# Output projection of blocks 1 to 8 by one level of Strassen's product, with the sums of h on VectorE

## Chip, cores, metric

The kernel runs on one core of one Trainium2 chip. The metric is device time in microseconds (us); quoted times are medians of several executions. The span in a profile is some 1.8 us shorter than the time of the same execution. Faster or slower is given at 2%.

## The reference

Linear attention over 8 batches of 8 heads, 576 rows of 64, then a GEGLU block on the 4608 x 512 result:

```python
q_s = softmax(q, axis=-1); k_s = softmax(k, axis=2)           # per head
x   = (q_s @ (k_s^T @ v)) laid out as 4608 x 512
g, val = x @ w_gate, x @ w_val                                # 512 -> 1536
out = (gelu(g) * val) @ w_out                                 # 1536 -> 512
```

## The kernel before

Rows are handled in blocks of 512: blocks 0 to 7 are one batch each (512 of its 576 rows), block 8 gathers the remaining 64 rows of all; the order is 0 to 6, 8, 7. A block runs 12 steps `fi` (128 of the 1536 hidden features each: four matmuls for the gate, four for the value, a gelu on ScalarE, a product on VectorE that writes the f16 slice `ht`) and then the output projection. The attention of later batches rides between these steps, by a plan `at(block, FI or NS, index, work)`; instructions of an engine run in program order. In the plan's names, exp and norm are the exponentials and the normalisation of a softmax, kv is the product of k and v, x that of q with kv, and FI or NS says whether the work rides behind a step `fi` or in the output projection.

```python
ps_big = tile_pool("ps_big", bufs=6, PSUM); ps_att = tile_pool("ps_att", bufs=2, PSUM)   # 8 banks
...
def gate(psg, psv):
    gl = ffn.tile([P, 512], f32, tag="gl")
    nc.scalar.activation(out=gl, in_=psg, func=ACTF.Gelu)
    ht = htp.tile([P, 512], f16, tag="ht")
    nc.vector.scalar_tensor_tensor(out=ht, in0=psv, scalar=_H_SCALE, in1=gl, op0=mult, op1=mult)
    return ht
...
def mm_out(psy, hts, ns, fis):
    for fi in fis:
        nc.tensor.matmul(psy, hts[fi][:, ns*P:(ns+1)*P], wo_sb[:, fi, :],
                         start=(fi == 0), stop=(fi == NFI - 1))
...
# plan, block 1 and later
at(1, FI, 3, L(exp, "q", 2), L(norm, 2, 0, "pool"))          # norm = reduce + reciprocal on VectorE,
...                                                          # multiply on GpSimd ("pool")
at(1, FI, 7, L(exp, "k", 2, 0, 4), L(cast_v, 2, 0, H))       # cast_v: f32 -> f16 on GpSimd
at(1, FI, 11, L(load_batch, 3), L(exp, "k", 2, 4, 8), L(exp, "q", 3), L(exp, "k", 3), ...)
at(1, NS, 0, L(unit_kv4, 2)); at(1, NS, 1, L(unit_x4, 2, ("dve", "dve"), 1))   # block 2's x
at(2, FI, 7, L(norm_rem0))
for b in range(2, B):
    at(b, FI, 0, L(load_batch, b + 2))
    at(b, FI, 11, L(exp, "q", b + 2), L(exp, "k", b + 2), L(cast_v, b + 2, 0, H))
    ...
# per block, b > 0
for ns in range(4):
    psy = ps_big.tile([P, C], f32, tag="mm")
    mm_out(psy, hts, ns, range(6));  ride(b, NS, 10 + ns)
    mm_out(psy, hts, ns, range(6, 12)); evac(b, ns, psy); ride(b, NS, ns)
```

The softmax here doesn't subtract the row's maximum and nothing guards it: scores larger than these inputs give would overflow.

## Time and profile before

| | before |
|---|---|
| time | 313.39 us (313.31 to 313.39, 3 runs) |
| TensorE / VectorE / ScalarE / GpSimd busy | 97 / 54 / 45 / 17% of the span of 311.7 us |
| output projection of one block | 48 matmuls of 512 columns, 10.4 us |

A group's row is: line, engine, operation, output <- inputs, shapes, count | busy us, mean ns of one | idle us just before, and what ended it. A timeline row is: start us, duration us, engine, line, operation, count, and in brackets the idle time before it with its releaser. A record of a matmul lasts longer than its share of a stream (379 ns for 216), because neighbours overlap. The lines themselves stand in the prediction.

### The profile page before, as it was taken

What the parts mean: (1) busy time and instruction counts of PE and PEld (TensorE: products, weight loads), DVE (VectorE), ACT (ScalarE), POOL (GpSimd) and SP (SyncE); (2) the same over time, 40 slices, a digit from 0 to 9 for tenths busy, and PEclk for the clock granted to TensorE, in tenths of its full rate; (3) what the DMA queues carried; (4) which work ended last, traced back from release to release, by engine and by line L of the source; (5) the groups of instructions that cost most, each with busy time, mean ns of one, the idle gap of its engine ahead of it and who ended that gap; (6) DMA issues with size and microseconds to landing.
All of it is one profiled execution on the core that took longest, in us unless ns stands there. A gap on an engine that the chain in (4) does not pass through costs nothing.

```text
span 311.7 us, 4689 instructions
## 1 busy us (share of the span) xinstructions
PE 302.9 (97%) x1813; PEld 140.6 (45%) x1813; DVE 168.8 (54%) x293; ACT 139.6 (45%) x181; POOL 54.0 (17%) x67
## 2 busy tenths in 40 slices
PE   3999999999999999999999999999999999999995
PEld 1544455444444444444444444444444444444444
DVE  2944386483686478437853686358643443324331
ACT  4763475994843743366335633474330333013300
POOL 2667451071083100110003000300000000000000
PEclk9999999999999999999999999999999999999999
DMA  7999999609999018901693149512210200140002
GB/s 227 372 383 393 401 386 388 182 2 262 375 337 241 0 69 269 334 14 67 191 349 69 67 127 386 97 43 93 54 33 34 103 0 0 36 101 0 0 36 101
DMA packets 55189, 51.61 MB, mean 166 GB/s; under 512 B 18560, under 2 KB 50688, under 8 KB 55168
## 3 DMA queue, kind: packets, MB, share of 16 engines
q1 hardware_dynamic: 53440, 49.68, 49.6%
q10 hardware_dynamic: 1728, 1.64, 1.7%
q8 instruction: 14, 0.23, 0.3%
q14 instruction: 7, 0.06, 0.1%
HBM read 37.75 MB, written 9.44 MB: 151 GB/s over the span
## 4 chain that ended last, share of the span: by engine, by line
PE 95%; DMA 2%; DVE 2%; ACT 0%; issue 0%; ACTq 0%
PE psg L406 30%; PE psv L406 30%; PE psy L481 29%; DMA qt<-in_q_dram 2%; PE pskv L281 1%; PE psl L502 1%; PE psx L369 1%; DVE rq L186 1%; PE psx L348 1%; DVE eq L195 0%; PE pskv L222 0%; PE pst L306 0%; PE psxr L369 0%; ACT eq L158 0%; PE pskv L258 0%; DVE eqt L138 0%
## 5 line engine op out<-in xcount | busy, mean ns | idle before, releaser
L411 ACT ACTIVATE gl<-psg 128x512 f32<-128x512 f32 x108 | 63.6, 598 | 122.9 <-PE psg L406 122.5
L413 DVE SCALAR_TENSOR_TENSOR ht<-psv,gl 128x512 f16<-128x512 f32 x108 | 74.0, 689 | 81.5 <-PE psv L406 77.4
L406 PE MATMUL psg<-xt,wg_sb 128*128 128x512 f16 x384 | 100.5, 379 | 0.0
L406 PE MATMUL psv<-xt,wv_sb 128*128 128x512 f16 x384 | 100.5, 379 | 0.0
L481 PE MATMUL psy<-wo_sb,ht 128*128 128x512 f16 x420 | 93.9, 379 | 0.0
L406 PEld LDWEIGHTS <-wv_sb 128*128 128x128 f16 x432 | 42.1, 98 | 50.8 <-issue 0.2
L406 PEld LDWEIGHTS <-wg_sb 128*128 128x128 f16 x432 | 42.1, 98 | 50.3
L481 PEld LDWEIGHTS <-ht 128*128 128x128 f16 x420 | 40.5, 98 | 48.4 <-issue 0.8
L530 DVE TENSOR_SCALAR yo<-psy 128x512 f32<-128x512 f32 x30 | 20.6, 688 | 32.4 <-PE psy L481 32.4
L134 POOL CAST v<-vt 128x640 f16<-128x640 f32 x26 | 18.2, 740 | 108.9 <-DMA vt<-in_v_dram 108.9
L176 DVE TENSOR_REDUCE rq<-eq 128x10 f32<-128x640 f16 x28 | 22.7, 811 | 5.4 <-ACT eq L158 4.9
L158 ACT ACTIVATE eq<-qt 128x2560 f16<-128x2560 f32 (+2 forms) x10 | 18.5, 1864 | 6.8 <-DMA qt<-in_q_dram 6.8
L158 ACT ACTIVATE ek<-kt 128x1280 f16<-128x1280 f32 (+1 forms) x11 | 19.1, 1747 | 3.9 <-DMA kt<-in_k_dram 3.8
L195 POOL TENSOR_TENSOR eq<-eq,rrq 128x640 f16<-128x640 f16 (+1 forms) x11 | 14.3, 1300 | 25.4 <-DVE rrq L178 17.1
L195 DVE TENSOR_TENSOR eq<-eq,rrq 128x640 f16<-128x640 f16 (+1 forms) x21 | 17.3, 822 | 0.2
L406 PE MATMUL psg<-xtr,wg_sb 128*128 128x512 f16 x48 | 12.3, 379 | 0.0
L406 PE MATMUL psv<-xtr,wv_sb 128*128 128x512 f16 x48 | 12.3, 379 | 0.0
L138 DVE CAST xt<-psx 128x512 f16<-128x512 f32 (+1 forms) x17 | 10.7, 668 | 2.0 <-PE psx L348 1.8
L398 PE MATMUL pswarm<-warm,ident 128*128 128x512 f16 x20 | 6.9, 501 | 4.9 <-ACT warm L553 4.9
L158 ACT ACT_TABLE_LOAD x8 | 10.3, 1283 | 0.8 <-DMA qt<-in_q_dram 0.7
L136 ACT CAST xt<-psx 128x512 f16<-128x512 f32 (+1 forms) x16 | 8.6, 574 | 2.4 <-PE psx L348 2.2
L136 ACT CAST xtr<-psxr 128x128 f16<-128x128 f32 (+1 forms) x6 | 1.6, 283 | 17.8 <-PE psxr L369 15.3
(67 smaller groups left out, 111.0 us busy)
## 6 DMA issues: line engine op xcount, KB each, us to landing
out_dram<-yo SPq DMA_DIRECT2D x12, 512.0 KB, 3.6
kt<-in_k_dram SPq DMA_DIRECT2D x7, 640.0 KB, 7.1
vt<-in_v_dram SPq DMA_DIRECT2D x7, 640.0 KB, 8.7
qt<-in_q_dram SPq DMA_DIRECT2D x7, 640.0 KB, 5.6
qt<-in_q_dram SPq DMA_DIRECT2D x8, 512.0 KB, 6.2
wost<-in_moe_w_out_dram SPq DMA_DIRECT2D x6, 512.0 KB, 7.9
kt<-in_k_dram SPq DMA_DIRECT2D x6, 512.0 KB, 7.8
vt<-in_v_dram SPq DMA_DIRECT2D x6, 512.0 KB, 9.4
```

Of the source, the lines that this page charges most:

```text
L134: nc.gpsimd.tensor_copy(out=dst, in_=src)
L136: nc.scalar.copy(out=dst, in_=src)
L138: nc.vector.tensor_copy(out=dst, in_=src)
L158: nc.scalar.activation(out=dst[:, n0:NC, h0 * D:h1 * D].rearrange(o, d=D, **({"t": 2} if b >= QUAD else {})), in_=heads(tiles[(nm, b)], b, ...
L176: nc.vector.reduce_sum(rq, e, axis=mybir.AxisListType.X)
L195: (nc.gpsimd if eng == "pool" else nc.vector).tensor_tensor(out=e, in0=e, in1=rrq.unsqueeze(-1).to_broadcast((P, n, 2, D)), op=ALU.mult)
L398: nc.tensor.matmul(ps, ident, warm, start=True, stop=True)
L406: nc.tensor.matmul(ps, w[:, ci, fi * P:(fi + 1) * P], xt[:, ci, :], start=(ci == 0), stop=(ci == HP - 1))
L411: nc.scalar.activation(out=gl, in_=psg, func=ACTF.Gelu)
L413: nc.vector.scalar_tensor_tensor(out=ht, in0=psv, scalar=_H_SCALE, in1=gl, op0=ALU.mult, op1=ALU.mult)
L481: nc.tensor.matmul(psy, hts[fi][:, ns * P:(ns + 1) * P], wo_sb[:, fi, :], start=(fi == 0), stop=(fi == NFI - 1))
L530: nc.vector.tensor_scalar(out=yo, in0=psy, scalar1=1.0 / _H_SCALE, scalar2=None, op0=ALU.mult)
```

## The change

Split h and w_out into halves along both axes. One level of Strassen's product (in Winograd's form, with shared sums) replaces 8 half-size products by 7, at the price of sums of h halves (four per pair of slices, on VectorE in each of blocks 1 to 8), sums of w_out halves (four, once, in block 1) and more traffic at the eviction. With h's halves a11 (features 0 to 5, rows 0 to 255), a12 (features 6 to 11), a21, a22 (the same for rows 256 to 511):

```diff
+    ring = [f"mm{i}" for i in range(6)]          # banks handed out in fixed turn; some held across products
+    ht = const.tile([P, NFI, 512], f16)          # one tile for all of h
+    def sum_w(i):                                # tw1 = b12-b11, tw2 = b22-tw1, tw3 = b22-b12, tw4 = b21-tw2
+        nc.vector.tensor_tensor(out=t, in0=a, in1=b, op=ALU.subtract)          # 128 x 1536 f16
+    def sum_h(j0, j1, which):                    # s1 = a21+a22, s2 = s1-a11, a21 <- a11-a21, s4 = a12-s2
+        for i in which: nc.vector.tensor_tensor(out=o, in0=a, in1=b, op=op)    # (j1-j0) x 256 f16
+    SUMS = {7: (0, 2), 9: (2, 4), 10: (4, 5)}    # after these fi; slice 5 after the last gate
+    def out_strassen(b, last):                   # a, c, b: PSUM banks; snap: scaled copy to SBUF
+        product(1, ps["a"], True);  s1 = snap("a"); sum_h(5, 6, (3, 4))
+        product(5, ps["c"], True);  s5 = snap("c")
+        product(6, ps["a"], False); s2 = snap("a"); ride(b, NS, 2)
+        product(3, ps["c"], False); add("c", s2, 0, 1)
+        product(7, ps["a"], False); add("a", s5, 1, 1); ride(b, NS, 4)
+        product(2, ps["b"], True);  add("b", s1, 0, 0); store_rows(b, 0, yo[0])
+        product(4, ps["a"], False)               # evicted by ScalarE
...
+    for i in range(4): at(1, FI, 3 + i, L(sum_w, i + 1))
-    at(1, NS, 0, L(unit_kv4, 2))
-    at(1, NS, 1, L(unit_x4, 2, ("dve", "dve"), 1))
+    at(1, NS, 2, L(unit_kv4, 2))
+    at(1, NS, 4, L(unit_x4, 2, ("act", "dve"), 1))
...
-                at(*((b, FI, hp) if n == 3 else (b - 1, NS, hp)), L(norm_sum, n, hp))
-                at(b, FI, hp, L(norm_mul, n, hp, "pool" if n == 3 else "dve"))
+                at(b, FI, hp, L(norm_sum, n, hp), L(norm_mul, n, hp, "pool"))
...
+            if b > 0 and fi in SUMS: sum_h(*SUMS[fi], (1, 2, 3, 4))
```

A product is 6 x 2 matmuls of 256 columns, so a block has 84 of them. Below, the seam of a block is the stretch from its last gates into its first products, where the last sums of h and the snaps are due.

More of the change, by code (lines that the diff above doesn't have):

```diff
@@ L56, with big, let_go, bank @@
     yop = ctx.enter_context(tc.tile_pool(name="yop", bufs=2))
-    htp = ctx.enter_context(tc.tile_pool(name="htp", bufs=13))
-    ps_big = ctx.enter_context(tc.tile_pool(name="ps_big", bufs=6, space=bass.MemoryType.PSUM))
+    ps_big = ctx.enter_context(tc.tile_pool(name="ps_big", bufs=1, space=bass.MemoryType.PSUM))
     ps_att = ctx.enter_context(tc.tile_pool(name="ps_att", bufs=2, space=bass.MemoryType.PSUM))
     ctx.enter_context(tc.manual_schedule())
+    ring = [f"mm{i}" for i in range(6)]
+    held = {}
+    def big(shape, dt, name, hold=False):
+        tag = ring.pop(0)
+        t = ps_big.tile(shape, dt, name=name, tag=tag)
+        if hold:
+            held[id(t)] = (t, tag)
+        else:
+            ring.append(tag)
+        return t
+    def let_go(t):
+        ring.append(held.pop(id(t))[1])
+    def bank(shape, name, spare):
+        return big(shape, f32, name) if spare else ps_att.tile(shape, f32, name=name, tag="att")
     warm = const.tile([P, 512], f16)
@@ L74 @@
     xtr = const.tile([P, HP, B * REM], f16)
+    ht = const.tile([P, NFI, 512], f16)
+    s4 = const.tile([P, NO, 256], f16)
     q0r = const.tile([64, H, D], f32)
@@ L240, in ksum_mm @@
     def ksum_mm(g):
-        st[("pks", g)] = ps_big.tile([P, 2], f32, name="pks", tag="mm")
+        st[("pks", g)] = big([P, 2], f32, "pks")
         for j in range(2):
@@ L252, in kv0_mm @@
     def kv0_mm(hp):
-        ps = ps_big.tile([P, D], f32, name="pskv0", tag="mm")
+        ps = big([P, D], f32, "pskv0")
         st[("pskv0", hp)] = ps
@@ L271, in unit_kv, with unit_kv4 @@
         kv_norm(b, g)
-    def unit_kv4(b, big=False):
-        ps = (ps_big if big else ps_att).tile([P, HP, VW], f32, name="pskv",
-                                              tag="mm" if big else "att")
+    def unit_kv4(b, spare=False):
+        ps = bank([P, HP, VW], "pskv", spare)
         for hp in range(HP):
@@ L342, in get_xt, with unit_x @@
         return st[(b, "xt")]
-    def unit_x(b, hp, eng="act", big=False):
+    def unit_x(b, hp, eng="act", spare=False):
         xt = get_xt(b)
-        psx = (ps_big if big else ps_att).tile([P, MAIN], f32, name="psx",
-                                               tag="mm" if big else "att")
+        psx = bank([P, MAIN], "psx", spare)
         nc.tensor.matmul(psx, st[(b, "kv", hp)].rearrange("p h e -> p (h e)"),
@@ L355, in unit_x_halves @@
             c = slice(i * MAIN // 2, (i + 1) * MAIN // 2)
-            psx = ps_big.tile([P, MAIN // 2], f32, name="psx", tag="mm")
+            psx = big([P, MAIN // 2], f32, "psx")
             nc.tensor.matmul(psx, st[(b, "kv", hp)].rearrange("p h e -> p (h e)"),
@@ L386, in unit_x4 @@
         for i in range(2):
-            ps = [ps_big.tile([P, MAIN], f32, name="psx", tag="mm") for _ in range(2)]
+            ps = [big([P, MAIN], f32, "psx") for _ in range(2)]
             for hp in (2 * i, 2 * i + 1):
@@ L391, in unit_x4 @@
                 copy_on(eng, xt[:, i + 2 * s, :], ps[s])
-    pswarm = ps_big.tile([P, 512], f32, name="pswarm", tag="mm")
+    pswarm = big([P, 512], f32, "pswarm")
     def warm_pe(n):
@@ L407, in mm_gv, with gate @@
                              start=(ci == 0), stop=(ci == HP - 1))
-    def gate(psg, psv):
+    def gate(psg, psv, fi):
         gl = ffn.tile([P, 512], f32, name="gl", tag="gl")
         nc.scalar.activation(out=gl, in_=psg, func=ACTF.Gelu)
-        ht = htp.tile([P, 512], f16, name="ht", tag="ht")
         nc.vector.scalar_tensor_tensor(
-            out=ht, in0=psv, scalar=_H_SCALE, in1=gl, op0=ALU.mult, op1=ALU.mult)
-        return ht
+            out=ht[:, fi, :], in0=psv, scalar=_H_SCALE, in1=gl, op0=ALU.mult, op1=ALU.mult)
     def ffn_fi(xt, fi, spare=False):
-        pool, tag = (ps_att, "att") if spare else (ps_big, "mm")
-        psg = pool.tile([P, 512], f32, name="psg", tag=tag)
+        psg = bank([P, 512], "psg", not spare)
         mm_gv(psg, wg_sb, xt, fi, range(HP))
-        psv = pool.tile([P, 512], f32, name="psv", tag=tag)
+        psv = bank([P, 512], "psv", not spare)
         mm_gv(psv, wv_sb, xt, fi, range(HP))
-        return gate(psg, psv)
+        gate(psg, psv, fi)
     def ffn_first(xt, after):
@@ L428, in ffn_first @@
         for fi in range(len(after)):
-            psg = ps_big.tile([P, 512], f32, name="psg", tag="mm")
-            psv = ps_big.tile([P, 512], f32, name="psv", tag="mm")
+            psg = big([P, 512], f32, "psg")
+            psv = big([P, 512], f32, "psv")
             if fi == 0:
@@ L443, in ffn_first @@
             mm_gv(psv, wv_sb, xt, fi, [2])
-        hts = []
         for fi, (psg, psv) in enumerate(ps):
@@ L447, in ffn_first @@
             mm_gv(psv, wv_sb, xt, fi, [3])
-            hts.append(gate(psg, psv))
-        return hts
+            gate(psg, psv, fi)
     def ffn_first0(xt, xs):
@@ L455, in ffn_first0 @@
             for nm in ("g", "v"):
-                ps[(nm, fi)] = ps_big.tile([P, 512], f32, name="ps" + nm, tag="mm")
+                ps[(nm, fi)] = big([P, 512], f32, "ps" + nm)
         def go(fi, cis):
@@ L469, in ffn_first0, with mm_out @@
         go(1, (2,))
-        hts = []
         for fi in range(2):
             go(fi, (3,))
-            hts.append(gate(ps[("g", fi)], ps[("v", fi)]))
-        return hts
+            gate(ps[("g", fi)], ps[("v", fi)], fi)
     yo_t = {}
     order = list(range(B - 1)) + [B, B - 1]
-    def mm_out(psy, hts, ns, fis):
+    def mm_out(psy, ns, fis):
         for fi in fis:
-            nc.tensor.matmul(psy, hts[fi][:, ns * P:(ns + 1) * P], wo_sb[:, fi, :],
+            nc.tensor.matmul(psy, ht[:, fi, ns * P:(ns + 1) * P], wo_sb[:, fi, :],
                              start=(fi == 0), stop=(fi == NFI - 1))
@@ L492, in store @@
                                   ap=[[pm, nm], [NM * pn, 2]] + last), in_=src)
-    def last_rows(b, hts, ns):
-        cuts = ((0, 256), (256, 384), (384, 512))
-        ps = [ps_big.tile([P, c1 - c0], f32, name="psl", tag="mm") for c0, c1 in cuts]
-        for part in ((0,), (1, 2)):
-            for fi in range(NFI):
-                for i in part:
-                    c0, c1 = cuts[i]
-                    nc.tensor.matmul(ps[i], hts[fi][:, ns * P:(ns + 1) * P], wo_sb[:, fi, c0:c1],
-                                     start=(fi == 0), stop=(fi == NFI - 1))
-            for i in part:
-                c0, c1 = cuts[i]
-                yl = yop.tile([P, c1 - c0], f32, name=f"yl{i}", tag=f"yl{i}", bufs=1)
-                if i < 2:
-                    nc.vector.tensor_scalar(out=yl, in0=ps[i], scalar1=1.0 / _H_SCALE,
-                                            scalar2=None, op0=ALU.mult)
-                else:
-                    nc.scalar.activation(out=yl, in_=ps[i], func=ACTF.Copy, scale=1.0 / _H_SCALE)
-                store(nc.scalar if i == 2 else nc.sync, yl, b, ns, ns + 1, c0, c1)
+    tw = {}
@@ new lines, in sum_w, with make_s @@
+    def sum_w(i):
+        t = wstp.tile([P, NO, 256], f16, name=f"tw{i}", tag="wst")
+        b11, b12 = wo_sb[:, 0:NO, 0:256], wo_sb[:, 0:NO, 256:512]
+        b21, b22 = wo_sb[:, NO:NFI, 0:256], wo_sb[:, NO:NFI, 256:512]
+        a, b = {1: (b12, b11), 2: (b22, tw.get(1)), 3: (b22, b12), 4: (b21, tw.get(2))}[i]
+        nc.vector.tensor_tensor(out=t, in0=a, in1=b, op=ALU.subtract)
+        tw[i] = t
+    sh = {}
+    def make_s():
+        for i in (1, 2):
+            sh[i] = wstp.tile([P, NO, 256], f16, name=f"sh{i}", tag="wst")
@@ new lines, in sum_h @@
+    def sum_h(j0, j1, which):
+        a11, a21 = ht[:, j0:j1, 0:256], ht[:, j0:j1, 256:512]
+        a12, a22 = ht[:, NO + j0:NO + j1, 0:256], ht[:, NO + j0:NO + j1, 256:512]
+        s1, s2 = sh[1][:, j0:j1], sh[2][:, j0:j1]
+        for i in which:
+            o, a, b, op = {1: (s1, a21, a22, ALU.add), 2: (s2, s1, a11, ALU.subtract),
+                           3: (a21, a11, a21, ALU.subtract),
+                           4: (s4[:, j0:j1], a12, s2, ALU.subtract)}[i]
+            nc.vector.tensor_tensor(out=o, in0=a, in1=b, op=op)
@@ new lines, with product @@
+    SUMS = {7: (0, 2), 9: (2, 4), 10: (4, 5)}
+    def product(i, ps, first, ts=(0, 1)):
+        for j in range(NO):
+            for t in ts:
+                c0, c1 = slice(t * P, (t + 1) * P), slice(256 + t * P, 256 + (t + 1) * P)
+                a = {1: ht[:, j, c0], 2: ht[:, NO + j, c0], 3: s4[:, j, c0], 4: ht[:, NO + j, c1],
+                     5: sh[1][:, j, c0], 6: sh[2][:, j, c0], 7: ht[:, j, c1]}[i]
+                w = {1: wo_sb[:, j, 0:256], 2: wo_sb[:, NO + j, 0:256],
+                     3: wo_sb[:, NO + j, 256:512]}.get(i)
+                if w is None:
+                    w = tw[{4: 4, 5: 1, 6: 2, 7: 3}[i]][:, j]
+                nc.tensor.matmul(ps[t], a, w, start=(first and j == 0 and (
+                    t == ts[0] or ps[t].tensor is not ps[ts[0]].tensor)),
+                                 stop=(j == NO - 1), skip_group_check=True)
@@ new lines, in out_strassen, with get, parts, snap @@
+    def out_strassen(b, last):
+        yo = [yop.tile([P, 2, C], f32, name="yo", tag="yo") for _ in range(2)]
+        c = (slice(0, 256), slice(256, 512))
+        ps, tiles_ = {}, {}
+        def get(nm):
+            if last:
+                tiles_[nm] = [big([P, 256], f32, "ps" + nm, True) for _ in range(2)]
+                ps[nm] = [x for x in tiles_[nm]]
+            else:
+                tiles_[nm] = [big([P, 2, 256], f32, "ps" + nm, True)]
+                ps[nm] = [tiles_[nm][0][:, t] for t in range(2)]
+        def parts(nm):
+            return [(0, ps[nm][0]), (1, ps[nm][1])] if last else [(slice(0, 2), tiles_[nm][0])]
+        def snap(nm):
+            sn = ffn.tile([P, 2, 256], f32, name="sn", tag="gl")
+            for n, (t, src) in enumerate(parts(nm)):
+                if n:
+                    nc.scalar.activation(out=sn[:, t], in_=src, func=ACTF.Copy, scale=1.0 / _H_SCALE)
+                else:
+                    nc.vector.tensor_scalar(out=sn[:, t], in0=src, scalar1=1.0 / _H_SCALE,
+                                            scalar2=None, op0=ALU.mult)
+            return sn
+        def add(nm, sn, half, col):
+            for t, src in parts(nm):
+                nc.vector.scalar_tensor_tensor(
+                    out=yo[half][:, t, c[col]], in0=src, scalar=1.0 / _H_SCALE,
+                    in1=sn[:, t], op0=ALU.mult, op1=ALU.add)
+        get("a")
+        product(1, ps["a"], True)
+        s1 = snap("a")
+        sum_h(NO - 1, NO, (3, 4))
+        get("c")
+        product(5, ps["c"], True)
+        s5 = snap("c")
+        product(6, ps["a"], False)
+        s2 = snap("a")
+        ride(b, NS, 2)
+        product(3, ps["c"], False)
+        add("c", s2, 0, 1)
+        for x in tiles_["c"]:
+            let_go(x)
+        product(7, ps["a"], False)
+        add("a", s5, 1, 1)
+        ride(b, NS, 4)
+        if last:
+            for t in range(2):
+                store(nc.sync, yo[1][:, t, c[1]], b, 2 + t, 3 + t, 256, 512)
+        get("b")
+        product(2, ps["b"], True)
+        add("b", s1, 0, 0)
+        store_rows(b, 0, yo[0])
+        for x in tiles_["b"]:
+            let_go(x)
+        for ts in ((0,), (1,)) if last else ((0, 1),):
+            product(4, ps["a"], False, ts)
+            if ts == (1,):
+                nc.vector.tensor_scalar(out=yo[1][:, 1, c[0]], in0=ps["a"][1],
+                                        scalar1=1.0 / _H_SCALE, scalar2=None, op0=ALU.mult)
+            else:
+                t, src = parts("a")[0]
+                nc.scalar.activation(out=yo[1][:, t, c[0]], in_=src, func=ACTF.Copy,
+                                     scale=1.0 / _H_SCALE)
+            if last:
+                store(nc.sync, yo[1][:, ts[0], c[0]], b, 2 + ts[0], 3 + ts[0], 0, 256)
+        for x in tiles_["a"]:
+            let_go(x)
+        if not last:
+            store_rows(b, 1, yo[1])
@@ L514, in evac, with store_rows @@
+    def store_rows(b, half, yo):
+        if b < B:
+            store(nc.sync, yo.rearrange("p n c -> p (n c)"), b, 2 * half, 2 * half + 2)
+            return
+        for t in range(2):
+            for j in range(2):
+                o = 2 * (2 * half + t) + j
+                nc.sync.dma_start(
+                    out=out[o * S:(o + 1) * S, :].rearrange("(m n) c -> m n c", n=NT)[:, 0, :],
+                    in_=yo[j * 64:(j + 1) * 64, t, :])
     def evac(b, ns, psy, eng="dve"):
@@ L517, in evac @@
         yo = yo_t[b][:, ns % 2, :]
-        if b == B:
-            nc.vector.tensor_scalar(out=yo, in0=psy, scalar1=1.0 / _H_SCALE,
-                                    scalar2=None, op0=ALU.mult)
-            for j in range(2):
-                nc.sync.dma_start(
-                    out=out[(2 * ns + j) * S:(2 * ns + j + 1) * S, :].rearrange(
-                        "(m n) c -> m n c", n=NT)[:, 0, :],
-                    in_=yo[j * 64:(j + 1) * 64, :])
-            return
         if eng == "act":
@@ L531, in evac @@
                                     scalar2=None, op0=ALU.mult)
-        if b in (B - 2, B - 1):
-            store(nc.sync, yo, b, ns, ns + 1)
-        elif ns % 2 == 1:
+        if ns % 2 == 1:
             store(nc.sync, yo_t[b].rearrange("p n c -> p (n c)"), b, ns - 1, ns + 1)
@@ L633 @@
     at(1, FI, 11, L(load_batch, 3), L(exp, "k", 2, 4, 8), L(exp, "q", 3), L(exp, "k", 3), L(exp_rem0), L(cast_v, 3, 0, H))
-    at(1, NS, 0, L(unit_kv4, 2))
-    at(1, NS, 1, L(unit_x4, 2, ("dve", "dve"), 1))
+    for i in range(4):
+        at(1, FI, 3 + i, L(sum_w, i + 1))
+    at(1, FI, 6, make_s)
+    at(1, NS, 2, L(unit_kv4, 2))
+    at(1, NS, 4, L(unit_x4, 2, ("act", "dve"), 1))
     at(2, FI, 7, L(norm_rem0))
@@ L649 @@
                 at(b, FI, 5, L(unit_kv4, n))
-            at(b, NS, 2, L(unit_x4, n, ("act", "dve"), 0 if n == 4 else None))
+            at(b, NS, 4, L(unit_x4, n, ("act", "dve"), 0 if n == 4 else None))
             if n + 1 < B:
-                at(b, NS, 2, L(unit_kv4, n + 1, n == 4))
+                at(b, NS, 4, L(unit_kv4, n + 1, n == 4))
     def ride(b, kind, i):
@@ L660 @@
         xt = get_xt(b) if b < B else xtr
-        hts = []
         fi0 = 0
         if b < 2:
-            hts = ffn_first0(xt, (x_upper0, L(unit_x, 0, 3, "dve"))) if b == 0 else ffn_first(xt, first1)
-            fi0 = len(hts)
+            if b == 0:
+                ffn_first0(xt, (x_upper0, L(unit_x, 0, 3, "dve")))
+            else:
+                ffn_first(xt, first1)
+            fi0 = 2 if b == 0 else 3
             ride(b, FI, fi0 - 1)
         for fi in range(fi0, NFI):
-            hts.append(ffn_fi(xt, fi, b == 1 and fi == 7))
+            ffn_fi(xt, fi, b == 1 and fi == 7)
             ride(b, FI, fi)
+            if b > 0 and fi in SUMS:
+                sum_h(*SUMS[fi], (1, 2, 3, 4))
         if b == 0:
@@ L672 @@
             for ns in range(4):
-                psys.append(ps_big.tile([P, C], f32, name="psy", tag="mm"))
-                mm_out(psys[ns], hts, ns, range(0, NFI // 2))
+                psys.append(big([P, C], f32, "psy"))
+                mm_out(psys[ns], ns, range(0, NFI // 2))
                 ride(b, NS, ns)
@@ L677 @@
                 cut = 9 if ns == 2 else 7 if ns == 3 else NFI
-                mm_out(psys[ns], hts, ns, range(NFI // 2, cut))
+                mm_out(psys[ns], ns, range(NFI // 2, cut))
                 ride(b, NS, 14 + ns)
-                mm_out(psys[ns], hts, ns, range(cut, NFI))
+                mm_out(psys[ns], ns, range(cut, NFI))
                 evac(b, ns, psys[ns], "act" if ns == 3 else "dve")
@@ L683 @@
         else:
-            for ns in range(4):
-                if b == order[-1] and ns == 3:
-                    last_rows(b, hts, ns)
-                    break
-                psy = ps_big.tile([P, C], f32, name="psy", tag="mm")
-                mm_out(psy, hts, ns, range(NFI // 2))
-                ride(b, NS, 10 + ns)
-                mm_out(psy, hts, ns, range(NFI // 2, NFI))
-                evac(b, ns, psy)
-                ride(b, NS, ns)
+            sum_h(NO - 1, NO, (1, 2))
+            out_strassen(b, b == order[-1])
 _INS = ['q', 'k', 'v', 'moe_w_gate', 'moe_w_val', 'moe_w_out']
```

## The prediction

> **What bounds the kernel now.** I read the page's busy shares and chain first, then the groups by shape, the waits, and the timeline around the output projection and around block 1.
>
> ```profile
> PE 302.9 (97%) x1813; PEld 140.6 (45%) x1813; DVE 168.8 (54%) x293; ACT 139.6 (45%) x181; POOL 54.0 (17%) x67
> PEclk9999999999999999999999999999999999999999
> PE 95%; DMA 2%; DVE 2%; ACT 0%; issue 0%; ACTq 0%
> ...
> L481 PE MATMUL psy<-wo_sb,ht 128*128 128x512 f16 x420 | 93.9, 379 | 0.0
> ```
>
> TensorE is busy 97% of the span, holds 95% of the chain that ended last, and its clock is full throughout. The output projection (psy) never waits. So any TensorE column removed is time removed, unless a new wait takes its place; VectorE, at 54%, has room on average. Two other stretches matter. The end of the last block, from the timeline, shows what narrow matmuls cost:
>
> ```profile
> 305.70 0.69 DVE L530 TENSOR_SCALAR yo<-psy 128x512 f32<-128x512 f32 x1 [1.90 <-PE psy L481]
> ...
> 307.01 0.42 DVE L508 TENSOR_SCALAR yl<-psl 128x256 f32<-128x256 f32 x1 [0.62 <-PE psl L502]
> ...
> 308.30 0.29 DVE L508 TENSOR_SCALAR yl<-psl 128x128 f32<-128x128 f32 x1 [0.86 <-PE psl L502]
> ```
>
> Between the first two evictions TensorE ran 12 matmuls of 256 columns, each with its own weight load: 1.31/12 = 109 ns each. Between the last two it ran 24 of 128: 54 ns each. A 512-column matmul takes 216 ns (the chain shows 36 in 7.77 us). So halving the width halves the cost almost exactly, and weight loads stay hidden.
>
> The other stretch is block 1, the only one in which VectorE, ScalarE, GpSimd and the loads are all late:
>
> ```profile
> 61.89 1.26 POOL L195 TENSOR_TENSOR eq<-eq,rrq 128x640 f16<-128x640 f16 x1 [13.07 <-DVE rrq L178]
> ...
> 71.91 1.31 SPq L114 DMA_DIRECT2D qt<-in_q_dram  x2
> ...
> 78.32 2.34 ACT L158 ACTIVATE eq<-qt 128x2560 f16<-128x2560 f32 x1 [4.97 <-DMA qt<-in_q_dram]
> ...
> 81.27 2.34 ACT L158 ACTIVATE ek<-kt 128x2560 f16<-128x2560 f32 x1 [0.60 <-DMA kt<-in_k_dram]
> ...
> 82.91 1.03 PE L406 MATMUL psg<-xt,wg_sb 128*128 128x512 f16 x4
> 83.11 0.69 DVE L530 TENSOR_SCALAR yo<-psy 128x512 f32<-128x512 f32 x1 [1.07 <-PE psy L481]
> 83.51 0.61 ACT L203 ACTIVATE eq0r<-q0r 64x512 f16<-64x512 f32 x1
> ```
>
> ScalarE, in order, waits there for block 3's loads and ends its exps at 84.1 us, after block 2's matmuls have begun at 82.9. Today that costs nothing because block 2's x is copied by VectorE alone.
>
> **What the Trainium skill says.** "TensorE: Matmul & The Clock Gate", section "Back-to-back issue gap", gives N/2.4 + 2.5 ns: 109 ns at 256 columns and 216 at 512, as the trace has it. The same section's sustained 131 ns for 512 columns and 81 ns for 128 do not fit this trace (216 and 54), so I use the trace. "VectorE: DVE Perf Modes", section on the perf-mode tier table, has tensor_tensor at two elements a cycle for 16-bit operands in SBUF and at one from PSUM. No such op is in the trace of before: its tensor_tensor on eq has a 4-byte operand and takes 0.82 us for 640 elements, one a cycle plus about 0.15. A 1024-element f16 copy from PSUM took 0.68 us, so two a cycle does occur. "SBUF — State Buffer", section "Who interferes with whom", says that a VectorE op with two SBUF inputs and a GpSimd op that reads SBUF lock each other out. The trace agrees in kind: four casts that ran while norm_rem0's multiply ran took 3.18 us, elsewhere 2.72.
>
> **The change part by part.**
>
> *Products.* A block's 48 matmuls of 512 columns cost 48 x 0.216 = 10.37 us. Seven products of 6 x 2 matmuls of 256 columns are 84 x 0.109 = 9.17 us. Gain 1.19 us a block; 8 blocks give 9.5 us, 3.0% of 313.39. That is the ceiling.
>
> *Sums of h.* Per block and sum, two ops of 512 elements and two of 256. Estimates from the skill's page and the trace's fixed 0.15 us: 0.42 and 0.29 us at two a cycle (0.69 and 0.42 at one), a group of four about 1.45 and 0.95 with the overlap of some 0.09 us that neighbouring VectorE ops show. So 1.45 us after fi 7 and fi 9, 0.95 after fi 10, and 4 ops of 0.29 at the seam: about 5 us a block. The pitch of one fi is 8 x 0.216 = 1.73 us, of which the gate takes 0.60 to 0.69. From the end of fi 7's matmuls (time 0): sums end 2.05, gate 8 2.65, gate 9 4.06, sums 5.5, gate 10 6.1, sums 7.05, gate 11 7.7, first two sums of j=5 8.25, snap of product 1 8.95. Product 6, which overwrites that bank, is due at 6.64 + 2.62 = 9.26. It just fits, with 0.3 us to spare. The three snaps and three adds (0.69 each) follow at one per product of 1.31 us and fit too.
>
> *Casts that land there.* GpSimd casts the next-but-one v when it lands, in blocks 2 to 5 about 8.4 fi into a block (98.9, 131.1, 164.3, 196.4 us). By the lock, one may hold up sums by 0.7 us or so each. Block 2 has norm_rem0 (1.65 us) at fi 7 besides. I take 0.8 us lost in block 2, 0.25 in each of 3 to 5, none in 6, 8 and 7: 1.5 us.
>
> *Multiplies moved to GpSimd.* They leave VectorE 3.3 us a block (4 x 0.82) and run at 1.26 each beside fi 0 to 4, where VectorE's ops have at most one SBUF input. The transpose then starts some 2 us later, and is needed 15 us later: free.
>
> *Block 1.* It gets the four weight sums (1536 elements, estimate 0.95 us each) at fi 3 to 6, where VectorE already has a gate, a reduction and a reciprocal (0.6 + 0.81 + 0.22, held back by ScalarE to 60.6 us), so each of these fis holds 2.6 us in a pitch of 1.73. Gate 7 moves from 67.3 to about 70.6, and the sums of fi 7 meet the last multiply and four casts on GpSimd. Gate 8 ends at 73 to 75; it frees the bank of psv 11, due at 70. Then TensorE stalls 3 to 5 us, and again about 1 at products 5 and 6, which need the sums. GpSimd's multiplies slip some 2 us, the transpose and behind it block 3's loads with them, so ScalarE's exps end near 86.5 rather than 84.1. Block 2's x is now copied by ScalarE too, behind those exps: 1.6 us (0.27, its second form, and two of 0.53). So block 2 starts at 85.7 even with no slip and near 88 with it, against 82.9. I take 4.2 us lost, block 1's own gain of 1.2 included.
>
> *The end.* P4's second half ends in 128x256 rather than 128x128 evictions (0.42 for 0.29), and its store queues behind a 512 KB one: 0.3 us.
>
> *Sum.* 7 x 1.19 = 8.3 gained; 4.2 + 1.5 + 0.3 = 6.0 lost. 313.4 - 2.3 = 311.1 us.
>
> **The rivals.** First, nearly the whole gain arrives: if block 1 costs only what ScalarE's exps force (2.8) and the seams nothing, 313.4 - 8.3 + 2.8 + 0.3 = 308.2, still under 2%; only if block 1 too is free would it be near 304. For it speaks VectorE's 54%; against it, block 1's timeline. Second, VectorE becomes the bound at the seam because the sums run at one element a cycle: sums after fi 7 to 10 are then some 7 us beside 2.8 of gates in 6.9, product 6 waits about 3 us a block, and the time is near 330. The skill's page speaks against it; nothing in the trace settles it. Third, the dependence of product 1 on all of h, now one tile: if it waited for gate 11, 1 us a block would go (about 318). Against it: block 0's first psy matmuls began at 36.8 us while wo_sb, one tile too, was still being cast at 38.7 to 42.8, so waits follow the slice. Fourth, weight loads bound the narrow matmuls: the 54 ns above speak against it.
>
> **Range and chances.** From 307.5 (first rival, a little better) to 315 (block 1 at 7 us and seams at 3). Faster than 307.1 needs block 1 nearly free: 0.13. Slower than 319.7 needs the second or third rival: 0.06. Within 2%: 0.81.
>
> **What would show it.** Right: 672 matmuls of 256 columns at 109 ns; sums of 512 elements at 0.42 us and of 256 at 0.29; TensorE idle in block 1 from about fi 11 on for gates and sums, and at block 2's start for a ScalarE copy of xt; waits of tenths of a us before product 6 in blocks 2 to 5; block 2 starting near 87 us, and each of the last blocks 1.2 us shorter. Wrong: sums at 0.69 us, TensorE waiting at every seam, or block 2 starting by 83 us.

## The result

The changed kernel takes **317.32 us** (317.2 to 317.53, 4 runs) against 313.39 for before: a ratio of 1.0125, 95% interval 1.011 to 1.0139: the same at 2%, though slower clear of the noise. It is correct. A ratio is the mean time of one kernel's runs over the mean of the other's of the same rounds, so not quite the ratio of the medians. The time lies above the predicted range (307.5 to 315.0), and on the other side of before.

The page of the changed kernel, busy shares, clock and chain:

```profile
PE 297.0 (94%) x2077; PEld 167.9 (53%) x2077; DVE 210.7 (67%) x424; ACT 146.0 (46%) x195; POOL 78.2 (25%) x83
PEclk9999999996999999999999999999999999999999
PE 79%; DVE 15%; issue 2%; DMA 2%; ACT 1%; DVEq 0%; ACTq 0%
```

TensorE has 5.9 us less to do, though part of it ran at a low clock (the 6), and the chain, which ran 95% through TensorE before, is now 15% VectorE. The view of waits names the places (us in total, times, longest):

```profile
PE psv L424 <- DVE ht L430: 4.5, 1, 4.5
PE psa L545 <- DVE sn L571: 2.0, 4, 0.5
PE psc L545 <- DVE sh L531: 1.4, 2, 1.1
PE pskv L278 <- DVE rck L270: 0.8, 1, 0.8
```

None of these four was there before. To place them I take each block from its first gate matmul to that of the next (the last: to the end of the span), read off the timeline:

| stage | before | after | difference | predicted |
|---|---|---|---|---|
| start to block 1 | 48.66 | 49.63 | +0.97 | 0 |
| block 1 | 34.25 | 40.04 | +5.79 | +4.2 |
| block 2 | 33.42 | 34.23 | +0.81 | -0.4 |
| block 3 | 32.68 | 32.37 | -0.31 | -0.94 |
| block 4 | 32.56 | 31.92 | -0.64 | -0.94 |
| block 5 | 32.56 | 32.50 | -0.06 | -0.94 |
| block 6 | 31.80 | 30.65 | -1.15 | -1.19 |
| block 8 | 31.08 | 29.93 | -1.15 | -1.19 |
| block 7 and the end | 34.68 | 34.16 | -0.52 | -0.89 |
| span | 311.7 | 315.4 | +3.7 | -2.3 |

Blocks 6 and 8 show the product as it should be: 1.15 us gained of an estimated 1.19. Nearly everything else is lost elsewhere. Block 1 in the timeline:

```profile
70.37 1.77 POOL L215 TENSOR_TENSOR eq<-eq,rrq 128x640 f16<-128x640 f16 x1 [0.63 <-PE psv L424]
70.94 0.68 DVE L430 SCALAR_TENSOR_TENSOR ht<-psv,gl 128x512 f16<-128x512 f32 x1
...
72.09 3.48 POOL L154 CAST v<-vt 128x640 f16<-128x640 f32 x4
73.20 0.93 DVE L531 TENSOR_TENSOR ht<-ht 128x512 f16<-128x512 f16 x1
...
74.91 1.28 DVE L430 SCALAR_TENSOR_TENSOR ht<-psv,gl 128x512 f16<-128x512 f32 x2
75.64 1.87 PE L424 MATMUL psv<-xt,wv_sb 128*128 128x512 f16 x4 [4.47 <-DVE ht L430]
77.30 2.77 PE L545 MATMUL psa<-wo_sb,ht 128*128 128x256 f16 x12
```

Gate 7 starts at 70.94 us, behind the weight sums; the sums after it run beside GpSimd's multiply and casts and take up to 0.93 us instead of 0.42; gate 8 (the first of the two at 74.91) frees the bank that TensorE has waited 4.47 us for. Then TensorE runs at half clock: product 1 starts 2.56 us before product 5 rather than 1.31. The multiply took 1.77 us on GpSimd where it took 1.26 before.

The seam of block 3, where the gain of 1.2 us shrank to 0.3:

```profile
138.71 0.42 DVE L531 TENSOR_TENSOR sh<-ht 128x512 f16<-128x512 f16 x1
139.06 3.28 POOL L154 CAST v<-vt 128x640 f16<-128x640 f32 x4 [4.19 <-DMA vt<-in_v_dram]
139.17 0.89 DVE L531 TENSOR_TENSOR sh<-sh,ht 128x512 f16<-128x512 f16 x1
139.98 0.93 DVE L531 TENSOR_TENSOR ht<-ht 128x512 f16<-128x512 f16 x1
...
148.12 1.47 PE L545 MATMUL psa<-tw,sh 128*128 128x256 f16 x12 [0.53 <-DVE sn L571]
```

The first sum, alone, took 0.42 us; those beside the casts 0.89 and 0.93. Nine us later product 6 waits for its snap. The queue on VectorE never caught up in between.

### The profile page after: what moved, and what is told of

Read it like the earlier page. It is cut to its first block, busy times and chain, and to the rows that moved or that the text cites. A ratio compares the mean times of both kernels' runs of the same rounds, so it can differ in the third digit from the quotient of the medians.

```text
span 315.4 us, 5395 instructions
## 1 busy us (share of the span) xinstructions
PE 297.0 (94%) x2077; PEld 167.9 (53%) x2077; DVE 210.7 (67%) x424; ACT 146.0 (46%) x195; POOL 78.2 (25%) x83
## 4 chain that ended last, share of the span: by engine, by line
PE 79%; DVE 15%; issue 2%; DMA 2%; ACT 1%; DVEq 0%; ACTq 0%
PE psv L424 26%; PE psg L424 25%; PE psa L545 12%; PE psc L545 5%; DVE sh L531 5%; DVE ht L430 4%; PE psb L545 4%; PE psy L492 3%; DMA qt<-in_q_dram 2%; DVE s L531 1%; PE pskv L300 1%; PE psx L387 1%; DVE sn L571 1%; DVE rq L206 1%; PE psx L366 0%
## 5 line engine op out<-in xcount | busy, mean ns | idle before, releaser
L215 POOL TENSOR_TENSOR eq<-eq,rrq 128x640 f16<-128x640 f16 (+1 forms) x27 | 36.7, 1360 | 112.8 <-DVE rrq L198 80.1
L545 PE MATMUL psa<-tw,ht 128*128 128x256 f16 x192 | 23.6, 273 | 0.0
L545 PEld LDWEIGHTS <-sh 128*128 128x128 f16 x192 | 18.7, 98 | 7.3 <-issue 2.7
L545 PE MATMUL psc<-tw,sh 128*128 128x256 f16 x96 | 12.6, 276 | 1.4 <-DVE sh L531 1.4
L531 DVE TENSOR_TENSOR sh<-ht 128x512 f16<-128x512 f16 (+1 forms) x32 | 13.1, 411 | 1.1
L531 DVE TENSOR_TENSOR sh<-sh,ht 128x512 f16<-128x512 f16 (+1 forms) x32 | 13.1, 410 | 1.1
L571 DVE TENSOR_SCALAR sn<-psa 128x512 f32<-128x512 f32 (+1 forms) x16 | 10.5, 654 | 4.9 <-PE psa L545 4.9
L545 PE MATMUL psa<-tw,sh 128*128 128x256 f16 x96 | 11.8, 272 | 2.0 <-DVE sn L571 2.0
L545 PE MATMUL psa<-wo_sb,ht 128*128 128x256 f16 x96 | 13.1, 291 | 0.0
L531 DVE TENSOR_TENSOR s<-ht,sh 128x512 f16<-128x512 f16 (+1 forms) x32 | 12.8, 399 | 0.0
```

Of the source, the lines that this page charges most:

```text
L215: (nc.gpsimd if eng == "pool" else nc.vector).tensor_tensor(out=e, in0=e, in1=rrq.unsqueeze(-1).to_broadcast((P, n, 2, D)), op=ALU.mult)
L531: nc.vector.tensor_tensor(out=o, in0=a, in1=b, op=op)
L545: nc.tensor.matmul(ps[t], a, w, start=(first and j == 0 and (t == ts[0] or ps[t].tensor is not ps[ts[0]].tensor)), stop=(j == NO - 1), ski ...
L571: nc.vector.tensor_scalar(out=sn[:, t], in0=src, scalar1=1.0 / _H_SCALE, scalar2=None, op0=ALU.mult)
```

## Experiments

All block lengths are from the profiled execution. Times of the variants that stall scatter by up to some 3 us from execution to execution, and their mean clock with them (e1: 315.37 us at 0.994, 318.27 at 0.986); so where block lengths and medians differ in detail, I trust the block lengths for places and the medians for totals. The block lengths scatter too: in the profiles of e1, e2, e3, e6 and e11, which leave blocks 3 to 5 as the change has them, the three together took 95.6 to 96.8 us, against 96.8 in the profile of the changed kernel.

### e1_start: a bank passed over at the start

```diff
     unit_x(0, 1, "act", True)
+    ring.append(ring.pop(0))
     kv0_mm(2)
```

> The changed kernel with one PSUM tag of the new ring passed over just before the third kv0 product of block 0, so that this product takes a bank that is already free. Theory (the new ring hands out the bank whose VectorE reciprocal comes later in program order, which before did not): the 0.84 us wait of TensorE at 15.8 us goes, block 0's first psy matmul starts at 36.8 us rather than 37.75, and the time falls by 0.9 to 1.0 us, from 317.3 to about 316.4. Rival (the late start is the scatter of one profile): nothing changes, 317.3.

Measured: 316.36 us (315.37 to 318.27), ratio 1.0096. The wait of 0.84 us at 15.8 us is gone, block 1 starts at 48.62 us (before: 48.66; changed kernel: 49.63). So the start's loss is the ring: it hands banks out in fixed turn, and the third kv0 product got the bank whose reader, a reciprocal, comes later on VectorE. Block 2 took 36.1 us in this profile rather than 34.2. It had nearly the same waits (1.26 and 0.53 us before matmuls of products 5 and 6, for 1.14 and 0.53), and after them the clock fell: products 6, 3 and 7 took 1.53, 2.55 and 1.60 us from start to start. This is the scatter named above; what decides whether the clock falls there stays open, for in block 2 of e5 it stayed at 1.00 after the same two waits.

### e2_warm: dummy matmuls in block 1's wait

```diff
+        if xt is st.get((1, "xt")) and fi == NFI - 1:
+            pd = ps_att.tile([P, 512], f32, name="pd", tag="att")
+            for _ in range(20):
+                nc.tensor.matmul(pd, ident, warm, start=True, stop=True)
         psv = bank([P, 512], "psv", not spare)
```

> The changed kernel with 20 dummy matmuls of 512 columns (4.3 us, into a spare bank that nobody reads) put where TensorE waits 4.5 us in block 1 for its last psv bank, so that TensorE's clock should not fall to half from 75 to 80 us. Theory (VectorE's backlog sets block 1's length; the slow clock runs beside it): the clock stays at 1.0, psv and product 1 take 0.86 and 1.31 us instead of 1.66 and 2.56, but products 5 and 6 then wait for sums and snap, and block 2 still starts within 0.5 us of 89.7; time 316.8 to 317.5. Rival (the fallen clock is a cost of its own): about 2.0 us less, 315.3.

Measured: 317.41 us (315.91 to 318.07), ratio 1.0117; the profiled execution is the fastest of them. The clock in the stretch from 75.0 to 80.1 us (columns: stretch, length, busy time and count by engine, clock, DMA share, GB/s), first the changed kernel, then this one:

```profile
75.00:80.10 5.10, 4.46 (x18) 2.49 (x18) 4.93 (x13) 3.15 (x3) 0.56 (x1) 0.50 0.95 239
```

```profile
75.00:80.10 5.10, 3.89 (x28) 2.46 (x26) 4.93 (x13) 3.15 (x3) 0.47 (x1) 1.00 0.94 241
...
80.31 0.39 PE L549 MATMUL psc<-tw,sh 128*128 128x256 f16 x2 [1.26 <-DVE sh L535]
81.23 1.47 PE L549 MATMUL psa<-tw,sh 128*128 128x256 f16 x12 [0.53 <-DVE sn L575]
```

The clock stayed at 1.00, yet block 1 took 39.96 us (40.04 without the dummies): the time won is waited away in front of products 5 and 6. VectorE was busy 4.93 of these 5.10 us in both. The low clock, tempting as an explanation, costs nothing measurable in block 1. (In block 2 of e1 and e6, where it fell after TensorE's waits for VectorE, the block was some 2 us longer.)

### e3_plain1: block 1 projected as before

```diff
-    for i in range(4):
-        at(1, FI, 3 + i, L(sum_w, i + 1))
+    for i, (kind, n) in enumerate(((FI, 7), (FI, 8), (NS, 10), (NS, 12))):
+        at(1, kind, n, L(sum_w, i + 1))
...                                              # kv4 and x4 of batch 2 at NS 0, 1; x by VectorE alone
-            if b > 0 and fi in SUMS:
+            if b > 1 and fi in SUMS:
...                                              # block 1: the loop over ns of before
```

> The changed kernel with block 1 projected as before (48 matmuls of 512 columns, no sums of h, rides and the copies of block 2's x by VectorE as before); the four weight sums are kept but moved to fi 7 and 8 and into block 1's projection. Theory (block 1's sums overload VectorE, worth 5.8 us net of block 1's own gain): block 1 takes 34 to 35 us instead of 40.0, the clock stays at 1.0, time 311.3 to 312.3. Rival (the loss sits at all seams alike, block 1 is only its first place): the stall moves to block 2 and at least 3 us of it stay, time above 314.

Measured: 312.3 us (311.77 to 313.92), ratio 0.9968. Block 1 took 34.53 us, and the stall did not move: block 2 took 34.33 (34.23 in the changed kernel), 3 to 5 took 32.2 to 32.3. So 5.5 us of block 1's length come from its sums and what goes with them (the run also gives up the seven products there and ScalarE's copies of x), and the four weight sums, which are still in the block, are nearly hidden once the sums of h are out of it and they no longer share a fi with a reduction.

### e4_casts: the casts of v on ScalarE

```diff
-            at(b, FI, NFI - 1, L(exp, "q", b + 2), L(exp, "k", b + 2), L(cast_v, b + 2, 0, H))
+            at(b, FI, NFI - 1, L(exp, "q", b + 2), L(exp, "k", b + 2))
+            at(b, FI, 9, L(cast_v, b + 2, 0, 4, "act"))
+            at(b, FI, 10, L(cast_v, b + 2, 4, 8, "act"))
```

> The changed kernel with the casts of v for batches 4 to 7, which land in the middle of the sums of blocks 2 to 5, moved from GpSimd to ScalarE (two at fi 9, two at fi 10). Theory (GpSimd's casts and VectorE's two-input sums lock each other out, and the delay reaches products 5 and 6): all sums of blocks 2 to 5 take 0.42 and 0.29 us, TensorE's waits at products 5 and 6 there fall below 0.2 us a block, blocks 3 to 5 become 0.4 to 0.8 us shorter and block 2 about 1 us, time 314.2 to 315.2. Rival (VectorE has too much work at the seam by itself): the sums get faster, the waits stay, time above 316.5.

Measured: 313.5 us (313.45 to 314.01), ratio 1.0002, 3.8 us below the changed kernel and more than expected. Block 3 in this kernel, sums and cast together:

```profile
140.83 0.42 DVE L531 TENSOR_TENSOR sh<-ht 128x512 f16<-128x512 f16 x1
141.29 0.42 DVE L531 TENSOR_TENSOR sh<-sh,ht 128x512 f16<-128x512 f16 x1
141.39 1.35 ACT L156 CAST v<-vt 128x640 f16<-128x640 f32 x2
141.63 0.42 DVE L531 TENSOR_TENSOR ht<-ht 128x512 f16<-128x512 f16 x1
...
145.94 1.47 PE L545 MATMUL psa<-tw,sh 128*128 128x256 f16 x12
```

A cast on ScalarE leaves the sums at 0.42 us, product 6 follows product 5 with no wait worth a mark, and blocks 3 to 5 take 31.53, 31.41 and 31.40 us: 1.15 us less than before the change, the same gain as in blocks 6 and 8. Block 2 fell to 33.00, where a wait is left:

```profile
114.54 1.47 PE L545 MATMUL psa<-tw,sh 128*128 128x256 f16 x12 [0.53 <-DVE sn L571]
```

So the loss at the seams of blocks 3 to 5 was the collision of VectorE's sums with GpSimd's casts, and VectorE's work alone just fits, as the prediction's queue had it.

### e5_spread: the sums spread evenly

```diff
-    SUMS = {7: (0, 2), 9: (2, 4), 10: (4, 5)}
+    SUMS = {6 + j: (j, j + 1) for j in range(5)}
```

> The changed kernel with the sums of h spread evenly: one of the five slices j after each of fi 6 to 10 (four ops of 256 elements, about 1 us) instead of two slices after fi 7 and fi 9 and one after fi 10. The casts stay on GpSimd. Theory (the seam is a queue on VectorE: a fi with 0.6 of gate and 1.4 or more of sums overruns its pitch of 1.73 us, and the backlog meets the casts): with 1.6 us in each fi the queue has room again by fi 11, TensorE's waits at products 5 and 6 fall below 0.3 us a block in blocks 3 to 5, and the time to 314 to 316 although the number of ops grows. Rival (only the casts matter, and they now meet even more ops): 317 or more. Block 1, overloaded by its weight sums, stays near 40 us under both.

Measured: 319.02 us (318.58 to 321.24), ratio 1.0191. A miss: block 1 41.63 us, blocks 3 to 5 32.0 to 32.4, no better than the change. One sum of 256 elements in block 1, against its usual 0.29:

```profile
70.93 1.34 DVE L531 TENSOR_TENSOR sh<-ht 128x256 f16<-128x256 f16 x1
```

It stood in line behind the rest of a 1.77 us multiply. What a short sum lost here, 1.05 us, is what was left of the GpSimd instruction, not a share of its own length. And the even spread leaves no slack: gates followed each other at 1.66 us (144.51, 146.17, 147.83) against a pitch of 1.73, so a delay is made good at 0.07 us a fi, while the original spacing leaves fi 8 free.

### e6_nosw and e7_nosums: without weight sums, without any sums (wrong results on purpose)

```diff
                 if w is None:
-                    w = tw[{4: 4, 5: 1, 6: 2, 7: 3}[i]][:, j]
+                    w = wo_sb[:, NO + j, 256:512]     # both; e7 also takes slices of ht for s1, s2, s4
...                                                    # sum_w (both) and sum_h (e7) emit nothing
```

> Wrong result on purpose: the changed kernel without the four weight sums (products 4 to 7 take a slice of wo_sb in their place); everything else as it is. Theory (the weight sums and the GpSimd multiplies and casts that lock with the sums each make a part of block 1's backlog): gate 7 ends 2.4 us earlier, TensorE waits some 2 us instead of 4.5 for the last psv bank, block 1 takes about 37.6 us instead of 40.0, time near 315. Rival (the weight sums alone make the backlog): block 1 falls to 35 us or less, time 312 or less.

Measured: 315.9 us (313.94 to 316.28), ratio 1.0064; block 1 took 37.60 us, as expected: taking out the weight sums takes 2.4 us off block 1. At most some 3 could have shown, because ScalarE's copies of x ended at 86.58 us and block 2 began at 87.08. The total came out 0.9 us above the expectation: block 2 took 36.24 us, with waits of 1.27 and 0.53 us and a fallen clock as in e1.

> Wrong result on purpose: the changed kernel with neither weight sums nor sums of h (the products take slices of ht and wo_sb instead); products, snaps, adds, rides and stores stay. It shows the TensorE side alone. Theory: products gain 1.15 to 1.2 us a block where nothing holds them up: blocks 2 to 5 at 32.2, 31.4, 31.4 and 31.4 us; block 1 still loses because block 2's x waits for the ScalarE copies behind the exps, so it takes some 36 to 37 us rather than 33.1; time 309 to 310.5. Rival (the seven products themselves cost more than 84 x 109 ns, by bank waits of snaps and adds): blocks 3 to 5 above 31.8 us.

Measured: 312.52 us (311.73 to 313.32), ratio 0.9969: with no sum at all, still hardly faster than before, and 2 us above the expectation. Blocks 3 to 5 took 31.49, 31.37 and 31.37 us, so the products themselves give what was predicted. Block 1 took 37.31, and block 2 34.68, 2.4 more than the 32.2 expected. The reason stands in the timeline, where block 2's first matmuls begin:

```profile
86.30 1.06 ACT L156 CAST xt<-psx 128x512 f16<-128x512 f32 x2
...
86.93 1.92 PE L424 MATMUL psg<-xt,wg_sb 128*128 128x512 f16 x4 [4.10 <-ACT xt L156]
```

TensorE waits 4.10 us for ScalarE's copies of x, which follow block 3's exps in ScalarE's order. Four matmuls then took 1.92 us for 1.03: the clock was 0.51 from 86.9 to 92.0 us. Here, with no queue on VectorE beside it, the low clock does cost time.

### e8_all: first combination

e1, e3, e4 and e5 together.

> A version meant to beat both, by the four causes found: Strassen's product from block 2 on only, block 1 plain with the weight sums at fi 7, 8 and in its projection; the passed-over tag at the start; the casts of v for batches 4 to 7 on ScalarE; the sums of h spread over fi 6 to 10. Theory (the four losses add up and nothing else takes their place): block 1 34.5 us, block 2 about 32.2, blocks 3 to 5 31.4, time 305.5 to 306.5, 2.2 to 2.5% under before. Rival (taking the waits away moves them, for instance to ScalarE's gelu behind the casts): 308 or more.

Measured: 307.08 us (306.97 to 307.17), ratio 0.9795 (0.9783 to 0.9808, unclear at 2%): 0.6 us above the expected range. Blocks 3 to 5 took 31.49, 31.37 and 31.37, as in e4 without the spread; block 2 took 33.18, with a wait of 0.53 before product 6: there norm_rem0 (1.56 us on VectorE at fi 7) stands among the evenly spread sums, and the gates and sums after it follow each other without a pause up to product 6's snap.

### e9_best: second combination

e1, e3 and e4 without the spread, and:

```diff
-    at(2, FI, 7, L(norm_rem0))
+    at(2, FI, 4, L(norm_rem0))
...
-                store(nc.sync, yo[1][:, ts[0], c[0]], b, 2 + ts[0], 3 + ts[0], 0, 256)
+                store(nc.scalar if ts[0] == 0 else nc.sync, yo[1][:, ts[0], c[0]], ...)
```

> The combined version again, with three differences: the sums of h stand after fi 7, 9 and 10 as in the change (the even spread did not help), norm_rem0 runs at fi 4 of block 2 instead of fi 7, where it shared VectorE with the sums, and in the last block the third-from-last store is issued by ScalarE's queue, so that the last one does not wait behind it. Theory (block 2 still loses about 1 us to a queue on VectorE that norm_rem0 starts, and the end 0.5 us to five issues of one queue): block 2 takes 32.1 to 32.3 us instead of 33.2, the end is 0.3 to 0.6 us shorter, time 305.4 to 306.1. Rival (block 2's extra microsecond is something else): 306.7 or more.

Measured: **306.46 us** (306.25 to 306.56), ratio 0.9772, 95% interval 0.9758 to 0.9785: faster than both kernels, though 0.4 us above the expectation. Block 2 took 32.26 us, as expected, and TensorE is busy without a gap from the start of block 2 to that of block 7 (in block 3, for instance, 31.53 us of 31.53). The spread was dropped and norm_rem0 moved in one step, but e4 tells which of the two freed block 2: there the sums are not spread, norm_rem0 is still at fi 7, and block 2 took 33.00 us with the wait of 0.53, although VectorE had stood idle for 1.03 us just before the gate of fi 7 and so carried nothing over. So it was norm_rem0's move. The end did not move (34.17 us, against 34.16 in e8): the last store was issued 0.03 us after the last eviction rather than 0.22, but took 2.59 us to land rather than 2.39. Issuing it earlier was no help, so what holds the end stays open; the last eviction ends 3.6 to 3.7 us before the span does, in before 3.1. Clock, block 3 (columns as in e2) and the first sum of this kernel:

```profile
PEclk9999999999999999999999999999999999999999
```

```profile
115.60:147.13 31.53, 31.53 (x247) 18.58 (x244) 22.64 (x48) 18.55 (x25) 5.03 (x4) 1.00 0.53 169
```

```profile
L531 DVE TENSOR_TENSOR sh<-ht 128x512 f16<-128x512 f16 x14 | 5.9, 425 | 0.5
```

### e10_nosums_xdve and e11_xdve: who copies block 2's x

```diff
-    at(1, NS, 4, L(unit_x4, 2, ("act", "dve"), 1))
+    at(1, NS, 4, L(unit_x4, 2, ("dve", "dve"), 1))      # e10: in e7; e11: in the changed kernel
```

> Wrong result on purpose: the kernel without any sums once more, with block 2's x copied by VectorE alone, as in the kernel before. Theory (with the sums gone, what is left of block 1's loss is TensorE's 4.1 us wait for ScalarE's copies behind the exps, and the clock that falls after that wait): block 1 takes 33.0 to 33.5 us instead of 37.3, block 2 about 32.3 instead of 34.7, time 305.8 to 306.8. Rival (the seven products themselves make block 1 long): block 1 stays above 35 us.

Measured: 306.52 us (306.26 to 306.63), ratio 0.9774, block 1 33.06 us. Its output is wrong, which doesn't matter for the time. Block 2 took 33.52 rather than 32.3: it waits 0.17 us for VectorE's copy of x and 0.64 for a gelu that follows the exps on ScalarE; the rest I have not traced. Both blocks together are 5.4 us below e7.

> The changed kernel with one difference: block 2's x is copied by VectorE alone, as in the kernel before, instead of ScalarE and VectorE. Theory (in the changed kernel VectorE's backlog ends later than ScalarE's chain, by some 0.6 us in the trace, so the copies behind the exps cost nothing here): block 1 stays at 39.5 to 41 us, time 316.8 to 318. Rival (the ScalarE copies are a cost of their own in the changed kernel): block 1 2 us or more shorter, time 315.3 or less.

Measured: 317.95 us (316.44 to 319.37), ratio 1.0139, block 1 40.15 us. So block 1 has two chains side by side: ScalarE's copies behind the exps would make it 37.3 us, VectorE's queue makes it 40.0, and removing the shorter one changes nothing.

## Why the prediction was wrong

The prediction had 8.3 us of gain and 6.0 of loss. The gain came: 1.15 us a block where nothing stands in the way (blocks 6 and 8; 3 to 5 in e4). The losses were mis-sized, in four terms.

- **Products, 1.19 us a block.** Right: 1.15. Weight loads stayed hidden (12 matmuls in 1.31 us).
- **Sums at two elements a cycle.** Right, and as the Trainium skill has it ("VectorE: DVE Perf Modes", section on the perf-mode tier table): 0.42 and 0.29 us undisturbed, weight sums 0.91 to 0.96. The rival of one element a cycle is out, and so is that of a wait for the whole of h: product 1 starts on the heels of the last value matmul.
- **"Casts that land there": 0.25 us in each of blocks 3 to 5, 0.8 in block 2.** This step failed most. The real losses against the gain of 1.19 are 0.88, 0.55, 1.13 and 2.0, in all 3.0 us more than the 1.5 I took; up to 1.2 us of it is the scatter of that one profile. I named the lock and the hour of the casts, but gave them a quarter of a us; in block 3 three sums in a row were stretched by some 0.5 each, and my own queue had 0.3 us to spare (none in block 3 of e4, where product 6 started 1.35 us after product 5 rather than 1.31). e4 takes the casts away and the whole of this loss in blocks 3 to 5 goes; of block 2's 2.0 it takes 1.2, and norm_rem0's move 0.7 more (e9).
- **Block 1, 4.2 us net.** Right in kind, and close in its steps: gate 7 at 70.94 (said: about 70.6), psv 11 waiting 4.5 us (said: 3 to 5), block 2's start moved. It came to 5.8, which is 1.6 more, and the path was another: I had ScalarE's copies of x behind the exps end last (85.7 us without a slip, near 88 with it, 87.1 taken) and TensorE wait for them at block 2's start. In the run these copies ended at 89.06, and TensorE came to block 2 at 89.67 without a wait, held up before by VectorE's queue. Both are 0.97 us late with the start. e7 and e10 show the copies' chain, a wait of 4.1 us once the sums are gone, but in the changed kernel it lies under VectorE's (e11). Of VectorE's part, the weight sums are 2.4 us (e6). The four sums after fi 7 took 3.3 us beside GpSimd's work, where the four after fi 9 of block 3 took 1.6; but no run takes GpSimd's work out of block 1, so the split of the rest is not shown.
- **The start.** Not foreseen at all: +0.97 us. I read the new ring as the old pool under another name. It is not: the old pool let the third kv0 product go ahead, the fixed turn does not (e1).
- **The end, 0.3 us.** 0.67 against the gain of 1.19; open, as told at e9.
- **The first rival, nearly the whole gain if block 1 costs only what the exps force,** named 308.2. e9, with those losses taken out one by one, reaches 306.5, because it gives up block 1's gain and with it its loss.

Added up: 3.0 (seams), 1.6 (block 1), 1.0 (start) and 0.4 (end) make 6.0 of the 6.2 us between 311.1 and 317.3.

## What to carry to other kernels

TensorE columns saved are time only where the engine that pays for them has room at that very hour: VectorE is at 67% of the span, and its queue, with ScalarE's copies hidden under it in block 1, still cost some 11 us (block 1 and blocks 2 to 5 against the gain of 1.15 us each). When two-input sums are added to VectorE, look for every GpSimd instruction that can run beside them, and count up to the length of that instruction for each sum it meets (here about 0.5 us beside casts of 0.68, and 1.05 behind a multiply); moving the casts to an engine with idle time was worth more than any reordering of the sums. When a loss has several chains side by side, take them away one at a time and then together, and watch the stage's length: here a fallen clock and a slow copy both looked like the cause of block 1's loss. The clock was not (e2), and the copy was only the next to come: without it block 1 stayed at 40.15 us, without the sums at 37.31, without both at 33.06.

## What the Trainium skill lacked or had wrong

- "SBUF — State Buffer", section "Who interferes with whom": right in kind, and the runs put sizes to it, which the page has not for this pair: a 512-element f16 sum 0.42 us alone, 0.89 to 0.93 beside casts of 0.68 us; a 256-element sum 0.29 us alone, up to 1.34 us behind a GpSimd multiply; and GpSimd pays too (the multiply 1.26 to 1.87 us, four casts 2.72 to 3.48).
- "TensorE: Matmul & The Clock Gate", section "Why this matters for your kernels", which advises against idle gaps above some 3 us: the clock also fell without one, after two waits of 1.26 and 0.53 us with matmuls between them (e1, mean clock 0.79 from 112 to 119 us), but not after the same two waits in e5; after the 4.47 us wait it was 0.50 for 5 us. The page speaks of frequent short idle times elsewhere, but has no figure for how short or how many.
- The same page, section "Back-to-back issue gap": its sustained 131 ns at 512 columns and 81 ns at 128, for streams with weight loads, do not hold here (216 and 56 ns from start to start, each matmul with its own load; the prediction's 54 was read between two evictions); its formula N/2.4 + 2.5 does, at 128, 256 and 512 columns (56, 109 and 216).
